# Attention and mixture of experts in one kernel: where the next head pair's q, k and v are moved, split and loaded

## The chip, the cores and the metric

The kernel runs on one core of a Trainium2 chip. The metric is the device time of one execution in microseconds (us), less is better. TensorE is PE in the profile, with its weight loads apart as PEld; VectorE is DVE, ScalarE is ACT, GpSimd is POOL, and SyncE is SP, whose queue (SPq) issues nearly all the DMAs.

## The reference

Attention over 2 batches of 8 heads, with 1152 keys of 64 values; queries are first averaged in twos, to 576 per head. Its output, as 1152 rows of 512, goes through 4 experts that are weighted with given probabilities.

```python
def _attn_ref(q, k, v):
    q_pool = q.reshape(B, H, S // 2, 2, D).mean(axis=3)
    scores = scale * np.matmul(q_pool, k.transpose(0, 1, 3, 2))
    attn = np.exp(scores - np.max(scores, axis=-1, keepdims=True))
    attn = attn / (np.sum(attn, axis=-1, keepdims=True) + 1e-09)
    return np.matmul(attn, v)
...
    p = domain_probs / (domain_probs.sum(-1, keepdims=True) + 1e-09)
    for e in range(E):
        h = np.maximum(x @ w1[e], 0.0)
        out += p[:, e:e + 1] * (h @ w2[e])
```

All is float32. Products that need more than one pass of TensorE take their operands as a rounded part (hi) and the rest (lo), each a tile of its own.

## The kernel before

**Pairs and periods.** Attention goes through 8 pairs of heads, n = 0 to 7. A pair has 9 tiles of 128 queries, and the program's main loop has one period for each, i = 0 to 8 (g = 9n + i counts them through). A period transposes one tile of exponentials (`T_chunk`, PE writes `pt`, DVE and ACT copy it to `aT`), does a part of the product with v (`PV_part`, PE writes `po`), and computes the scores of a tile that is three ahead (`scores`, PE writes `spt`; two ahead in pair 0), whose maximum DVE takes at once (L356) and whose exponentials ACT makes (L362). So the first scores of pair n+1 are computed in period 6 of pair n. Tile 8 holds the last 64 queries of both heads, and its scores are 9 matmuls of 384 columns (L327); the others' are L345 from pair 1 on, and read both halves of the partitions at once.

**Preparing a pair.** While pair n runs, pair n+1 is made ready, and pair n+2 is loaded:

- `load_q`, `load_kv` load q, k and v from HBM (SPq L169, L173).
- `add_q` adds neighbouring queries on POOL, `join_k` copies k to where it is transposed from (POOL L263).
- `prep_q` transposes q and the last eighth of k (PE writes `pq`), ACT copies them to `raw`, and POOL splits them into hi and lo (`pool_split`, L209 and L210): first the four full tiles, to a staging tile `stq`, then `split_q2m`, q's last tile, in four operations of 64 x 64, then k's. `move_q` takes each half of `stq` to the partitions where the scores read it, with two DMAs (SPq L282).
- `prep_k` does the same for k in two parts, `c` = 1 and 2 (PE writes `pk`); `stack_k` copies each to the other half of the partitions, two DMAs for each part (SPq L274, `kk<-kk`).

In pairs 1 and later `prep_k` stands in periods 1 and 3, `prep_q` in period 8 (for n+2); in pair 0 they stand in periods 3 to 5.

**x.** In periods 3 and 8 a product with v is complete. `finish` scales it on DVE (L428, tile `xr`) and splits the result on POOL for the experts (`xa` or `xb`), which read it after all pairs.

**Order.** All engines run their instructions in the order in which the program writes them, and so does the SP queue, where each wait holds up what stands behind it. In `S_rows` one matmul of a tile must be finished before another starts, and this is passed on by an empty instruction on SP (`relay`, L349) in every full tile from g = 13.

Of the kernel before, what the change touches and what calls it, by code (L numbers as in the profile page):

```python
# [8 lines left out]
F32 = mybir.dt.float32  # L9
F32R = mybir.dt.float32r  # L10
AF = mybir.ActivationFunctionType
ALU = mybir.AluOpType
# [5 lines left out]
def attention_moe_kernel(ctx, tc, q, k, v, probs, w1, w2, out):  # L18
    nc = tc.nc
    B, H, S, D = q.shape  # L20
    NT, DM = out.shape
    E, _, FF = w1.shape
    P = 128
    HALF = 64
# [40 lines left out]
    def xop(op, z, kt):  # L65
        if op in ("A11", "A12"):
            return xa[:, int(op == "A12"), z, kt, :]
        j = XI[op]
        if kt == 0:
            return xb[:, j, z, :]  # L70
        if j < 4 or z == 0:
            return q2all[:, (2 * j + z) * HT:(2 * j + z + 1) * HT]
        return kk[0][:, 3584:3584 + HT]
# [69 lines left out]
    with ExitStack() as actx:  # L143
# [12 lines left out]
        pr = ap.tile([P, 2 * 9, E], F32, name="pr")  # L156
        prs = ap.tile([P, 2 * 9], F32, name="prs")

        for t in q2m:
            nc.gpsimd.memset(t[:HALF, :, HALF:].bitcast(F32), 0.0)  # L160
            nc.gpsimd.memset(t[HALF:, :, :HALF].bitcast(F32), 0.0)

        pairs = [(b, hp) for b in range(B) for hp in range(NPAIR)]
        NP = len(pairs)
# [18 lines left out]
        def add_q(eng):  # L183
            eng.tensor_tensor(
                qsum[:, :8].rearrange("p (j y) d -> p y j d", y=2),
                qn[:, :8, 0, :].rearrange("p (y j) d -> p y j d", y=2),
                qn[:, :8, 1, :].rearrange("p (y j) d -> p y j d", y=2), ALU.add)
            eng.tensor_tensor(
                qsum[:, 8:], qn[:, 8:, 0, :].to_broadcast([P, 2, D]), qn[:, 8:, 1, :].to_broadcast([P, 2, D]), ALU.add)

        TCH = [(0, 5), (5, 9)]
        ROWS = [slice(0, HALF), slice(HALF, P)]
# [15 lines left out]
        def pool_split(hi, lo, src):  # L208
            nc.gpsimd.tensor_scalar(hi, src, 1.0, 1.0, ALU.mult, ALU.mult)  # L209
            nc.gpsimd.tensor_tensor(lo, src, hi.bitcast(F32), ALU.subtract)  # L210
# [11 lines left out]
        def prep_q0():  # L222
            pt = transposes_q0(range(4, 9))
            src = raw[:, :10 * HALF].rearrange("p (a k x) -> p a k x", a=2, x=HALF)
            nc.vector.tensor_copy(src, pt)
            pool_split(*parts_q0(1), src[:, :, :4])
            split_q2m(0, src)

        def split_q2m(n, src):
            for a, r in enumerate(ROWS):  # L230
                pool_split(q2m[n % 2][r, 0, r], q2m[n % 2][r, 1, r], src[r, a, 4])

        def half_of(h, z):
            return z if h else 1 - z
# [49 lines left out]
        def prep_q(n):  # L284
            pt = half_transposes("pq", [qsum[:, 2 * j:2 * j + 2].rearrange("p t d -> p (t d)") for j in range(5)] + [kc[0]])
            src = raw[:, :6 * P].rearrange("p (a k x) -> p a k x", a=2, x=HALF)
            nc.scalar.activation(src, pt, AF.Copy)
            pool_split(stq[:, 0], stq[:, 1], src[:, :, :4])
            if n == 1:
                for y in range(2):  # L290
                    move_q(n, y)
            split_q2m(n, src)
            ab = kab[n % 2]
            pool_split(halves(ab[:, 0], 8, 9)[:, :, 0], halves(ab[:, 1], 8, 9)[:, :, 0], src[:, :, 5])

# [126 lines left out]
        def finish(n, grp, po):  # L422
            b, hp = pairs[n]
            w, kt = GW[grp], hp % 2
            c = slice(256 * grp, 256 * grp + w)
            c1 = slice(HT + 256 * grp, HT + 256 * grp + w)
            x = xr[:, hp, c1 if b else c]
            nc.vector.tensor_tensor(x, po[:, :w], rb[grp], ALU.mult)  # L428
            if b == 0:
                op = "A12" if hp > 1 else "A11"  # L430
                pool_split(xop(op, 0, kt)[:, c], xop(op, 1, kt)[:, c], x)
                return
            a11, a12, a21 = xr[:, kt, c], xr[:, kt + 2, c], xr[:, kt, c1]
            if hp < 2:
                nc.gpsimd.tensor_tensor(a11, a11, x, ALU.subtract)
                if hp == 0:
                    split_x("S3", 0, c, a11, nc.gpsimd)
                return
            eng = nc.vector if hp == 3 else nc.gpsimd
            eng.tensor_tensor(a11, x, a11, ALU.subtract)  # L440
            todo = [("S2", a11), ("S1", a21), ("A22", x), ("S4", a12)]
            if eng is nc.gpsimd:
                eng.tensor_tensor(a21, a21, x, ALU.add)
                eng.tensor_tensor(a12, a12, a11, ALU.subtract)
                for op, src in todo:
                    split_x(op, kt, c, src, eng)
                return
            hi, lo = split_parts(todo[0], kt, c)
            hi()
            eng.tensor_tensor(a21, a21, x, ALU.add)  # L450
            eng.tensor_tensor(a12, a12, a11, ALU.subtract)
            rest = [split_parts(t, kt, c) for t in todo[1:]]
            late.append([lo] + [r[1] for r in rest])
            late.append([r[0] for r in rest])
            if grp == 0:
                for fn in late.pop() + late.pop():
                    fn()
# [5 lines left out]
                    lambda: nc.vector.tensor_tensor(lo, src, hi.bitcast(F32), ALU.subtract))  # L463

        late = []

        def scores(g):
            if g < NTL:
# [43 lines left out]
                 4: (0, 0, 0, 2), 5: (0, 0, 2, 4), 6: (0, 0, 4, 6), 7: (0, 0, 6, 8), 8: (0, 0, 8, 9)}  # L512
        SPREAD = {7: (0, 0), 2: (-1, 1)}
        PREP = {1: [(prep_k, 1)], 3: [(prep_k, 2)]}
        PREP0 = {3: [(prep_q,)], 4: [(prep_k, 1)], 5: [(prep_k, 2)]}

        def pv_part(g):
            n, i = divmod(g, 9)
# [18 lines left out]
        for g in range(NTL):  # L537
            n, i = divmod(g, 9)
            if i == 6 and n + 2 < NP:
                add_q(nc.gpsimd)  # L540
                join_k(0)
            if i == 7 and n + 2 < NP:
                join_k(1)
            if g == 2:
                load_q(2)
            if g == NTL - 1:
                nc.scalar.activation(UT["m1"], chx[:, :2, :CW], AF.Copy)
            for c in range(2):
                T_chunk(g, c)
            if g <= NQT:  # L550
                exps(g + 1)
            if i == 0 and n:
                inv_sums(n - 1, 1)
            if i == 4:
                inv_sums(n, 0)
            if g == NTL - 1:
                inv_sums(n, 1)
            if NQT < g < NTL - 2 and i not in (3, 8):
                exps(g + 2)
            if g == NQT:  # L560
                PV_part(0, 1, 0, 1)
                scores(g + 2)
                exps(g + 2)
                PV_part(0, 1, 1, 3)
            else:
                pv_part(g)
            if i in SPREAD and n + SPREAD[i][0] >= 0:
                spread_sums(n + SPREAD[i][0], SPREAD[i][1])
            if g == 0:
                prep_q0()  # L570
            if n + 1 < NP:
                for fn, *args in (PREP if n else PREP0).get(i, []):
                    fn(n + 1, *args)
                if i == 8 and n + 2 < NP:
                    prep_q(n + 2)
                if g == 5:
                    load_kv(kn, k, 2)
            elif i == 7:
                chx = ps_s.tile([P, 3, 512], F32, tag="s", name="chx")
                for kt in range(2):  # L580
                    product(0, 0, kt, chx, True)
            elif i == 8:
                for kt in range(2):
                    product(0, 2, kt, chx, False)
            if NQT <= g < NTL - 2 and i in (3, 8):
                exps(g + 2)
            scores(g + 2 if g < NQT else g + 3)
            if n and n + 1 < NP:
                if i == 0 and n + 2 < NP:
                    load_q(n + 2)  # L590
                if i in (1, 3):
                    move_q(n + 1, i // 2)
                if i in (2, 4):
                    stack_k(n + 1, *KST[i // 2 - 1])
                if i == 2 and n + 2 < NP:
                    load_kv(kn, k, n + 2)
                if i == 5:
                    load_kv(vn[(n + 1) % 2], v, n + 1)
            if g == 0:
                stack_k0()  # L600
                add_q(nc.gpsimd)
                join_k(0)
                join_k(1)
            if (n, i) == (1, 4):
                gate_weights()
            if (n, i) == (NP - 2, 4):
                load_w1(0)
            if (n, i) == (NP - 2, 7):
                w1_sums(0)
            if n == NP - 1:  # L610
                if i == 0:
                    split_x("S3", 1, slice(0, HT), xr[:, 1, :HT], nc.gpsimd)
                    load_w2(0)
                if i < 4:
                    w1_hi(0, WCH[i:i + 1])
                    w1_lo(0, WCH[i:i + 1])
                if i == 3:
                    load_w1(1)
                if i == 5:
                    w1_sums(1)  # L620
# [156 lines left out]
```

## Time and profile before

| | |
|---|---|
| Time, median of 3 runs | 632.39 us (630.92 to 633.32) |
| The profiled execution | 632.08 us, of which the span from first to last instruction is 629.9 us |
| PE busy | 608.2 us (97% of the span) |
| POOL busy | 346.9 us (55%) |
| DVE, ACT busy | 370.2 us, 292.9 us |
| DMAs on the SP queue | 48.94 MB |

Attention takes about the first 259 us of the span, the experts the rest. Times of rows are counted from the first instruction. The profiled execution is one, and its time lies 0.31 us under the median.

### The profile page before, as it was taken

What the parts mean: (1) busy time and instruction counts of PE and PEld (TensorE: products, weight loads), DVE (VectorE), ACT (ScalarE), POOL (GpSimd) and SP (SyncE); (2) the same over time, 40 slices, a digit from 0 to 9 for tenths busy, and PEclk for the clock granted to TensorE, in tenths of its full rate; (3) what the DMA queues carried; (4) which work ended last, traced back from release to release, by engine and by line L of the source; (5) the groups of instructions that cost most, each with busy time, mean ns of one, the idle gap of its engine ahead of it and who ended that gap; (6) DMA issues with size and microseconds to landing.
All of it is one profiled execution on the core that took longest, in us unless ns stands there. A gap on an engine that the chain in (4) does not pass through costs nothing.

```text
span 629.9 us, 12429 instructions
## 1 busy us (share of the span) xinstructions
PE 608.2 (97%) x5036; PEld 512.0 (81%) x5036; DVE 370.2 (59%) x571; ACT 292.9 (47%) x467; POOL 346.9 (55%) x415
## 2 busy tenths in 40 slices
PE   7889999999999999999999999999999999999997
PEld 6667677676777776889989989989989989989975
DVE  6657787786868777554454454454454454454444
ACT  5656667666667773635235235235225235224120
POOL 2655364543546498686476476476467467467040
PEclk8999999999999999999999999999999999999999
DMA  6574574928363521121121121121111111110105
GB/s 225 133 202 114 107 185 111 208 75 192 92 167 87 129 69 35 33 68 35 34 67 34 36 66 33 41 62 33 47 56 35 50 51 34 50 51 2 34 0 151
DMA packets 41337, 50.91 MB, mean 81 GB/s; under 512 B 3264, under 2 KB 27072, under 8 KB 41280
## 3 DMA queue, kind: packets, MB, share of 16 engines
q1 hardware_dynamic: 40480, 48.94, 29.9%
q10 hardware_dynamic: 800, 1.18, 0.5%
q8 instruction: 40, 0.66, 0.5%
q14 instruction: 17, 0.14, 0.1%
HBM read 30.97 MB, written 2.36 MB: 53 GB/s over the span
## 4 chain that ended last, share of the span: by engine, by line
PE 80%; DVE 6%; DMA 5%; POOL 3%; issue 2%; ACT 2%; SPq 0%; DVEq 0%; ACTq 0%
PE p L733 31%; PE chy L135 11%; PE chx L135 8%; PE chz L135 8%; PE po L391 7%; PE spt L345 7%; PE pt L202 4%; DMA kk<-kk 4%; DVE sx L356 3%; PE spt L327 2%; DMA kq<-in_k_dram 1%; POOL kk L210 1%; PE pq L202 1%; PE pr L202 1%; POOL kk L209 1%
## 5 line engine op out<-in xcount | busy, mean ns | idle before, releaser
L733 PE MATMUL p<-w2s,hb 128*128 128x512 f32 (+1 forms) x870 | 199.2, 388 | 1.1 <-DVE acc L737 0.9
L733 PEld LDWEIGHTS p<-w2s,hb 128*128 128x128 f32 x870 | 161.7, 188 | 34.3 <-issue 1.3
L737 DVE SCALAR_TENSOR_TENSOR acc<-p,pw,acc 128x512 f32<-128x512 f32 (+1 forms) x136 | 101.5, 747 | 82.7 <-PE p L733 82.7
L116 POOL TENSOR_TENSOR kk<-kq,kk 128x512 fp32r<-128x512 f32 x64 | 72.4, 1160 | 117.8 <-ACT kk L108 117.8
L356 DVE TENSOR_SCALAR_CACHE_REDUCE sx<-spt 128x1152 f32<-128x1152 f32 x72 | 97.7, 1357 | 53.6 <-PE spt L345 25.2
L362 ACT ACTIVATE sx<-sx,mn 128x1152 f32<-128x1152 f32 x72 | 90.5, 1257 | 22.5 <-DVE sx L356 22.4
L391 PE MATMUL po<-aT,vn 128*64 128x320 f32 (+1 forms) x576 | 85.5, 418 | 0.0
L664 POOL TENSOR_TENSOR hb<-xr,hb 128x576 fp32r<-128x576 f32 x48 | 68.7, 1433 | 21.9 <-ACT hb L663 21.9
L701 ACT ACTIVATE xr<-chx 128x576 f32<-128x576 f32 x15 | 9.8, 651 | 147.5 <-PE chx L135 147.5
L345 PE MATMUL spt<-kk,q2all 64*128 64x512 f32 (+1 forms) x504 | 65.1, 366 | 5.7 <-DMA kk<-kk 4.8
L345 PEld LDWEIGHTS spt<-kk,q2all 64*128 64x128 f32 x504 | 54.5, 186 | 18.5 <-DVE sx L356 6.4
L378 ACT ACTIVATE aT<-pt 128x640 f32<-128x640 f32 x72 | 50.5, 701 | 39.1 <-PE pt L202 39.0
L202 PEld LDWEIGHTS pt<-ident,sx 64*128 64x128 f32 x1296 | 55.5, 141 | 5.7 <-issue 3.5
L202 PE MATMUL pt<-ident,sx 64*128 64x64 f32 x1296 | 59.1, 227 | 0.5 <-ACT xr L304 0.4
L135 PE MATMUL chx<-xa,kk 128*128 128x288 f32 x384 | 56.5, 296 | 0.8 <-ACT xr L701 0.5
L135 PEld LDWEIGHTS chx<-xa,kk 128*128 128x128 f32 x384 | 53.4, 188 | 2.8 <-issue 0.9
L391 PEld LDWEIGHTS po<-aT,vn 128*64 128x64 f32 x576 | 35.0, 136 | 19.8 <-issue 0.2
L376 DVE COPY aT<-pt 128x512 f32<-128x512 f32 x72 | 49.3, 685 | 2.6 <-PE pt L202 2.6
L95 POOL TENSOR_TENSOR kq<-kq 128x256 f32<-128x256 f32 x64 | 45.8, 736 | 7.8 <-DMA kq<-in_moe_w_dram 6.7
L662 ACT ACTIVATE xr<-xr 128x576 f32<-128x576 f32 x48 | 32.9, 685 | 34.1 <-DVE xr L660 34.0
L135 PE MATMUL chy<-xb,kk 128*128 128x288 f32 x288 | 46.6, 297 | 0.5 <-ACT xr L670 0.3
L135 PE MATMUL chy<-q2all,kk 128*128 128x288 f32 x256 | 44.1, 294 | 0.0
(105 smaller groups left out, 726.9 us busy)
## 6 DMA issues: line engine op xcount, KB each, us to landing
kq<-in_moe_w_dram SPq DMA_DIRECT2D x64, 128.0 KB, 2.4
qsf<-in_moe_w_dram SPq DMA_DIRECT2D x16, 512.0 KB, 3.7
q2all<-q2all SPq DMA_DIRECT2D x28, 256.0 KB, 4.1
vn<-in_v_dram SPq DMA_DIRECT2D x8, 576.0 KB, 6.6
kk<-kk SPq DMA_DIRECT2D x14, 320.0 KB, 6.0
kq<-in_q_dram SPq DMA_DIRECT2D x7, 576.0 KB, 3.7
kq<-in_k_dram SPq DMA_DIRECT2D x7, 576.0 KB, 6.9
kk<-kk SPq DMA_DIRECT2D x14, 256.0 KB, 3.8
```

The lines of the kernel that those rows point to most:

```text
L116: nc.gpsimd.tensor_tensor(flat(w1s[u % 2][:, 1, a:b]), flat(wf[:, a:b]), flat(w1s[u % 2][:, 0, a:b].bitcast(F32)), ALU.subtract)
L135: nc.tensor.matmul(chain[:, c, :CW], w1s[u % 2][:, a, WI[wo], kt, :], xop(xo, z, kt)[:, c * CW:(c + 1) * CW], start=(first and kt == 0 and ...
L202: nc.tensor.transpose(pt[:, a, j, :], src[r], ident[r, r])
L345: mm = nc.tensor.matmul(sp[:, cs[c]], q2[n % 2][r, zq, h, ts_], src[n % 2][r, zk, cs[c]], start=(zq + zk == 0), stop=(zq == 1), skip_group ...
L356: nc.vector.tensor_scalar(sx[g % 3].rearrange("p (c x) -> p c x", c=3), spt.pop(g), -INV, None, ALU.mult, ALU.min, accum_out=mn[g % 3])
L362: nc.scalar.activation(sx[g % 3], sx[g % 3], AF.Exp, bias=mn[g % 3], scale=-1.0, accum_out=sums[n % 2][:, i:i + 1])
L376: nc.vector.tensor_copy(dst, pt)
L378: nc.scalar.activation(dst, pt, AF.Copy)
L391: nc.tensor.matmul(po[h * HALF:(h + 1) * HALF, :w], vn[n % 2][:, h, kt, :], aT[grp][:, h, kt, :], start=(kt == 0), stop=(kt == KT - 1))
L664: nc.gpsimd.tensor_tensor(lo, c, hi.bitcast(F32), ALU.subtract)
L733: nc.tensor.matmul(pc, h[:, a, sl, ts_], w[:, b, sl, c0:c1], start=(m == 0), stop=(m == len(ops) - 1))
L737: nc.vector.scalar_tensor_tensor(ac, pc, pw[:, tt, e:e + 1], ac, ALU.mult, ALU.add)
```

## The change

Four things are written in another order, and one is computed otherwise.

1. Where the result is split for the experts on POOL, `finish` puts it into a list, `behind`, that the main loop empties after the period's `prep_q` or `prep_k`. The last two heads' own path, on DVE, stays where it was.
2. `move_q` stands in periods 0 and 1 (before: 1 and 3), the first ahead of `load_q`; k of pair n+2 is loaded in period 4, behind the second `stack_k` (before: period 2, behind the first). `join_k(0)` is written in period 7.
3. `split_q2m` is gone: `add_q` writes the last tile's sums only into the half where they belong, the other half is set to zero once in `prep_q0`, and one split of 128 x 128 writes q's last tile with its zeros. Two of the four memsets at the start go.
4. In pair 0, `prep_q` and both `prep_k` stand in periods 2, 3 and 4.

```diff
-            eng.tensor_tensor(
-                qsum[:, 8:], qn[:, 8:, 0, :].to_broadcast([P, 2, D]), qn[:, 8:, 1, :].to_broadcast([P, 2, D]), ALU.add)
+            for a, r in enumerate(ROWS):
+                eng.tensor_tensor(qsum[r, 8 + a], qn[r, 8, 0, :], qn[r, 8, 1, :], ALU.add)
...
-            split_q2m(0, src)
-
-        def split_q2m(n, src):
             for a, r in enumerate(ROWS):
-                pool_split(q2m[n % 2][r, 0, r], q2m[n % 2][r, 1, r], src[r, a, 4])
+                pool_split(q2m[0][r, 0, r], q2m[0][r, 1, r], src[r, a, 4])
+                nc.gpsimd.memset(qsum[r, 9 - a], 0.0)
...
-            split_q2m(n, src)
+            pool_split(*(q2m[n % 2][:, z].rearrange("p (a x) -> p a x", a=2) for z in range(2)), src[:, :, 4])
...
-                pool_split(xop(op, 0, kt)[:, c], xop(op, 1, kt)[:, c], x)
+                behind.append(lambda: pool_split(xop(op, 0, kt)[:, c], xop(op, 1, kt)[:, c], x))
...
-                nc.gpsimd.tensor_tensor(a11, a11, x, ALU.subtract)
+                behind.append(lambda: nc.gpsimd.tensor_tensor(a11, a11, x, ALU.subtract))
...
-        PREP0 = {3: [(prep_q,)], 4: [(prep_k, 1)], 5: [(prep_k, 2)]}
+        PREP0 = {2: [(prep_q,)], 3: [(prep_k, 1)], 4: [(prep_k, 2)]}
...
             if i == 6 and n + 2 < NP:
                 add_q(nc.gpsimd)
+            if i == 7 and n + 2 < NP:
                 join_k(0)
-            if i == 7 and n + 2 < NP:
                 join_k(1)
...
+            while behind:
+                behind.pop(0)()
             if NQT <= g < NTL - 2 and i in (3, 8):
                 exps(g + 2)
             scores(g + 2 if g < NQT else g + 3)
             if n and n + 1 < NP:
+                if i < 2:
+                    move_q(n + 1, i)
                 if i == 0 and n + 2 < NP:
                     load_q(n + 2)
-                if i in (1, 3):
-                    move_q(n + 1, i // 2)
                 if i in (2, 4):
                     stack_k(n + 1, *KST[i // 2 - 1])
-                if i == 2 and n + 2 < NP:
+                if i == 4 and n + 2 < NP:
                     load_kv(kn, k, n + 2)
                 if i == 5:
                     load_kv(vn[(n + 1) % 2], v, n + 1)
```

The SP queue through one pair (n = 2) before: q's load, the first half of q's move, the first part of k's, k's load, q's second half, k's second part, v's load.

```order
L169 DMA kq<-in_q_dram 128x1152
L282 DMA q2all<-q2all 64x4x256 x2
L274 DMA kk_74<-kk_74 64x2x512 x2
L173 DMA kq<-in_k_dram 128x2x576
L282 DMA q2all<-q2all 64x4x256 x2
L274 DMA kk_74<-kk_74 64x2x640 x2
L173 DMA vn_89<-in_v_dram 128x2x576
```

The same stretch after (the changed file's lines are a few lower):

```order
L279 DMA q2all<-q2all 64x4x256 x2
L168 DMA kq<-in_q_dram 128x1152
L279 DMA q2all<-q2all 64x4x256 x2
L271 DMA kk_74<-kk_74 64x2x512 x2
L271 DMA kk_74<-kk_74 64x2x640 x2
L172 DMA kq<-in_k_dram 128x2x576
L172 DMA vn_89<-in_v_dram 128x2x576
```

All eight moves now stand ahead of the loads of k and v.

POOL in periods 1 to 4 of the same pair before: k's first part is joined and split (`kk`, hi and lo), then the result of the pair before for the experts (`xa`), then k's second part, and `spread`, which serves the sums of the exponentials.

```order
L263 COPY qsf<-kq 128x512
L209 TENSOR_SCALAR kk_74<-raw 128x512
L210 TENSOR_TENSOR kk_74<-raw,kk_74 128x512
L209 TENSOR_SCALAR xa<-xr 128x320
L210 TENSOR_TENSOR xa<-xr,xa 128x320
L209 TENSOR_SCALAR kk_74<-raw 128x512
L210 TENSOR_TENSOR kk_74<-raw,kk_74 128x512
L402 COPY spread<-rs_104 128x256
```

And after:

```order
L260 COPY qsf<-kq 128x512
L208 TENSOR_SCALAR kk_74<-raw 128x512
L209 TENSOR_TENSOR kk_74<-raw,kk_74 128x512
L208 TENSOR_SCALAR kk_74<-raw 128x512
L209 TENSOR_TENSOR kk_74<-raw,kk_74 128x512
L208 TENSOR_SCALAR xa<-xr 128x320
L209 TENSOR_TENSOR xa<-xr,xa 128x320
L399 COPY spread<-rs_104 128x256
```

The two operations on `xa` moved from ahead of k's second split to behind it.

PE in pair 0 before, from the transposes (`pt`) of period 2 on: q's preparation (`pq`) in period 3, k's first part (`pk`) in period 4, its second further on.

```order
L202 MATMUL pt<-ident,sx_92 128x64 x18
L327 MATMUL spt<-kk_73,q2all 128x384 x6
L202 MATMUL pt<-ident,sx_90 128x64 x18
L202 MATMUL pq<-ident,qsf 128x64 x10
L202 MATMUL pq<-ident,raw 128x64 x2
L327 MATMUL spt<-kk_73,q2all 128x384 x6
L202 MATMUL pt<-ident,sx_91 128x64 x18
L391 MATMUL po<-aT_93,vn_88 64x256 x4
L202 MATMUL pk<-ident,qsf 128x64 x8
L327 MATMUL spt<-kk_73,q2all 128x384 x6
```

And after, from the same transposes on:

```order
L201 MATMUL pt<-ident,sx_92 128x64 x18
L201 MATMUL pq<-ident,qsf 128x64 x10
L201 MATMUL pq<-ident,raw 128x64 x2
L324 MATMUL spt<-kk_73,q2all 128x384 x6
L201 MATMUL pt<-ident,sx_90 128x64 x18
L201 MATMUL pk<-ident,qsf 128x64 x8
L324 MATMUL spt<-kk_73,q2all 128x384 x6
L201 MATMUL pt<-ident,sx_91 128x64 x18
L388 MATMUL po<-aT_93,vn_88 64x256 x4
L201 MATMUL pk<-ident,qsf 128x64 x8
```

Each of the three preparations moved up by one period; the number of PE's instructions is the same.

## Rows read from the trace of the kernel before

**Rows 1.** Windows: length, busy us of five engines, clock, DMA share, GB/s.
```profile
12.60:45.22 32.62, 27.90 (x314) 21.27 (x315) 20.30 (x33) 20.19 (x30) 16.73 (x29) 0.91 0.74 191
62.87:91.63 28.76, 27.40 (x358) 20.36 (x355) 22.77 (x42) 19.24 (x30) 14.51 (x27) 1.00 0.60 139
91.63:118.82 27.19, 26.97 (x358) 20.24 (x355) 22.25 (x39) 19.22 (x30) 13.74 (x24) 1.00 0.62 149
118.82:147.32 28.50, 27.37 (x358) 20.36 (x355) 22.27 (x39) 19.25 (x30) 13.82 (x24) 1.00 0.60 145
147.32:176.42 29.10, 27.59 (x357) 20.44 (x354) 21.54 (x39) 19.21 (x30) 14.38 (x25) 1.00 0.59 138
176.42:204.87 28.45, 27.37 (x358) 20.37 (x355) 21.37 (x39) 19.25 (x30) 14.10 (x22) 1.00 0.48 110
```

**Rows 2.** Waits of PE: for whom, us in total, times, longest.
```profile
PE spt L345 <- DMA kk<-kk: 4.8, 5, 1.3
...
PE pq L202 <- POOL raw L263: 1.1, 1, 1.1
```

**Rows 3.** Timeline of pair 4, periods 3 to 8.
```profile
144.03 0.60 ACT L304 ACTIVATE raw<-pk 128x512 f32<-128x512 f32 x1 [1.22 <-PE pk L202]
144.31 0.46 POOL L209 TENSOR_SCALAR xa<-xr 128x320 fp32r<-128x320 f32 x1 [3.63 <-DVE xr L428]
144.85 0.87 POOL L210 TENSOR_TENSOR xa<-xr,xa 128x320 fp32r<-128x320 f32 x1
145.69 0.63 POOL L209 TENSOR_SCALAR kk<-raw 128x512 fp32r<-128x512 f32 x1
146.39 1.13 PE L345 MATMUL spt<-kk,q2all 64*128 64x512 f32 x9
146.40 1.29 POOL L210 TENSOR_TENSOR kk<-raw,kk 128x512 fp32r<-128x512 f32 x1
146.85 0.86 DVE L400 TENSOR_SCALAR rs<-sums 128x4 f32<-128x4 f32 x1
147.71 1.24 SPq L274 DMA_DIRECT2D kk<-kk  x2
149.27 1.51 PE L327 MATMUL spt<-kk,q2all 128*128 128x384 f32 x7 [0.16 <-DVE sx L356]
...
154.56 1.06 PE L345 MATMUL spt<-kk,q2all 64*128 64x128 f32 x8 [1.29 <-DMA kk<-kk]
159.94 0.25 PE L202 MATMUL pq<-ident,raw 64*128 64x64 f32 x2
```

**Rows 4.** DMAs from 141 us to 149.5 us, pair 4.
```profile
DMA packets 1323, 1.88 MB, mean 221 GB/s; under 512 B 97, under 2 KB 798, under 8 KB 1322
...
kk<-kk SPq DMA_DIRECT2D x2, 320.0 KB, 7.1
kq<-in_k_dram SPq DMA_DIRECT2D x1, 576.0 KB, 7.6
...
kk<-kk SPq DMA_DIRECT2D x2, 256.0 KB, 3.6
```

**Rows 5.** Timeline of pair 5: the same DVE operation, and POOL's beside it.
```profile
175.77 0.62 POOL L209 TENSOR_SCALAR kk<-raw 128x512 fp32r<-128x512 f32 x1
175.99 0.42 DVE L400 TENSOR_SCALAR rs<-sums 128x4 f32<-128x4 f32 x1
```

**Rows 6.** Timeline of pair 0.
```profile
21.04 0.29 POOL L263 COPY raw<-kq 128x128 f32<-128x128 f32 x1
21.72 1.31 PE L327 MATMUL spt<-kk,q2all 128*128 128x384 f32 x6 [0.80 <-DVE sx L356]
...
37.76 1.00 SPq L173 DMA_DIRECT2D kq<-in_k_dram  x1
43.97 0.29 POOL L263 COPY raw<-kq 128x128 f32<-128x128 f32 x1 [5.86 <-DMA kq<-in_k_dram]
44.31 0.28 PE L202 MATMUL pq<-ident,raw 64*128 64x64 f32 x2 [1.11 <-POOL raw L263]
```

More of the change, by code (lines that the diff above doesn't have):

```diff
@@ L157, in attention_moe_kernel @@
         prs = ap.tile([P, 2 * 9], F32, name="prs")
-        for t in q2m:
-            nc.gpsimd.memset(t[:HALF, :, HALF:].bitcast(F32), 0.0)
-            nc.gpsimd.memset(t[HALF:, :, :HALF].bitcast(F32), 0.0)
+        nc.gpsimd.memset(q2m[0][:HALF, :, HALF:].bitcast(F32), 0.0)
+        nc.gpsimd.memset(q2m[0][HALF:, :, :HALF].bitcast(F32), 0.0)
         pairs = [(b, hp) for b in range(B) for hp in range(NPAIR)]
@@ L434, in finish, with sums, all_split @@
             if hp < 2:
-                nc.gpsimd.tensor_tensor(a11, a11, x, ALU.subtract)
+                behind.append(lambda: nc.gpsimd.tensor_tensor(a11, a11, x, ALU.subtract))
                 if hp == 0:
-                    split_x("S3", 0, c, a11, nc.gpsimd)
+                    behind.append(lambda: split_x("S3", 0, c, a11, nc.gpsimd))
                 return
-            eng = nc.vector if hp == 3 else nc.gpsimd
-            eng.tensor_tensor(a11, x, a11, ALU.subtract)
             todo = [("S2", a11), ("S1", a21), ("A22", x), ("S4", a12)]
-            if eng is nc.gpsimd:
+            def sums(eng):
                 eng.tensor_tensor(a21, a21, x, ALU.add)
                 eng.tensor_tensor(a12, a12, a11, ALU.subtract)
+            def all_split(eng):
+                eng.tensor_tensor(a11, x, a11, ALU.subtract)
+                sums(eng)
                 for op, src in todo:
                     split_x(op, kt, c, src, eng)
+            if hp == 2:
+                behind.append(lambda: all_split(nc.gpsimd))
                 return
+            nc.vector.tensor_tensor(a11, x, a11, ALU.subtract)
             hi, lo = split_parts(todo[0], kt, c)
             hi()
-            eng.tensor_tensor(a21, a21, x, ALU.add)
-            eng.tensor_tensor(a12, a12, a11, ALU.subtract)
+            sums(nc.vector)
             rest = [split_parts(t, kt, c) for t in todo[1:]]
@@ L465, in attention_moe_kernel @@
         late = []
+        behind = []
         def scores(g):
```

## The prediction

> **What bounds the kernel now.** I read the windows first. Cut from period 5 of one pair to period 5 of the next, the five stretches do the same work, and PE is busy for 27.0 us to 27.6 us in each. But only one lasts as little as 27.19 us; the others last 28.76, 28.50, 29.10 and 28.45 us, all at full clock [rows 1]. So PE bounds attention, and four pairs hold 1.3 us to 1.9 us more than PE's work. The waits of PE say what that is: five waits for `kk<-kk`, the second part of k's move to the other half of the partitions, and one for POOL's copy L263 in front of q's preparation [rows 2]. The experts behind are 370 us of nearly unbroken matmuls that none of the edits touches: what attention saves should come off the end.
>
> Pair 4 shows how the wait arises [rows 3]. ACT delivers k's transposed second part at 144.63 (144.03 + 0.60). POOL is then busy with `xa`, which nobody needs before the experts, and takes k up at 145.69; its lo part ends at 147.69, and the SP queue issues the move at 147.71. PE, in period 6, starts the next pair's first tile and finds the move missing from 153.27 to 154.56. The move is not only issued late, it is slow: the two DMAs of k's second part took 7.1 us, while the two of its first part, 256 KB instead of 320 KB, took 3.6 us [rows 4]. What differs is what was issued ahead of them: k's load of 576 KB and q's second half.
>
> **The change part by part.**
>
> *Split and loads behind k's move.* With `xa` behind it, k's split can begin at 144.63, 1.06 us sooner, and ends at 146.63. The issue gains less: SP first has to pass on a matmul of the tile that starts at 146.39 and ends at 147.52 [rows 3]; I take 147.0. Ahead of this move there is now only k's first part, two periods older. Its transfer is bounded below by the 3.6 us of the smaller moves and above by 7.1 us; I take 4.5 us, which is 3.6 x 320 / 256, since nothing else is in flight ahead of it. It lands at 151.5, 1.8 us before PE asks, and the wait goes whole. What comes next in that place is known from the one stretch without it: 27.19 us [rows 1]. The gain is the excess over that stretch: 1.57 + 1.31 + 1.91 + 1.26 = 6.05 us. Bounds: 0 and 6.05.
>
> [...]
>
> *q moved in periods 0 and 1, q loaded behind its first half.* The same number of DMAs, each of which now waits at SP only for a split that POOL has finished about then; behind it in the queue stand empty instructions that PE waits for. Two DMAs take SP 1.24 us to issue, in a period of some 3 us (27.19 / 9) [rows 1, 3]. I cost it at nothing; if POOL were late by a microsecond PE would lose what exceeds the rest of the period, so 0 to +1 us over the kernel.
>
> *q's last tile in two operations instead of four, two additions instead of one.* All on POOL, which is busy for 14 us of 27 us in a pair [rows 1], and away from the path once `xa` is behind. Nothing.
>
> *A small DVE operation.* `rs` (L400), four columns wide, took 0.86 us in pair 4, from 146.85 to 147.71, beside POOL's lo operation that ended at 147.69; in pair 5, beside a shorter POOL operation, it took 0.42 us and ended as that one did [rows 3, 5]. Behind it PE waits 0.16 us for DVE [rows 3]. Pairs 1 to 4 have this pattern. With k's lo finished at 146.63, `rs` meets `xa`'s first operation (0.46 us) and should take about 0.42 us. That frees 0.16 us of PE four times: 0.64 us. Bounds: 0, and 0.44 x 4 = 1.8 us.
>
> *Pair 0.* Preparing a period earlier ends two waits: the pair's wait for `kk<-kk`, one of five that make 4.8 us, so about 1.0 us, and the wait of 1.11 us for POOL's copy, which waited 5.86 us for k's load [rows 2, 6]. That load was issued at 37.76 behind the moves; with them a period (3 us) sooner it lands before the copy is asked for. There is a price: in period 2 q's transposes now stand ahead of the scores that started at 21.72, and POOL's copy that they need ended at 21.33 (21.04 + 0.29) [rows 6]. Two memsets and a second addition come ahead of that copy. From POOL's other small operations I take 0.8 us, so the transposes (0.28 us) end near 22.4 and the scores start 0.7 us late; some of it comes back in period 5, which loses a preparation. I take 0.5 us. Sum for pair 0: 1.0 + 1.1 - 0.5 = 1.6 us gained; bounds 0 and 2.6.
>
> *The sum.* 6.05 + 0.64 + 1.6 = 8.3 us. Against the profiled execution's 632.08 us that is 623.8 us; the median of the runs is 0.31 us above that execution, so I say **624.0 us**.
>
> **The rivals.**
>
> *The moves stay half as slow.* If transfers share the engines whatever their order, k's load (1.3 us behind) and v's take a part from the moves. The 640 KB of the moves would have 1.3 us alone at 221 GB/s (0.29 MB), and the other 0.37 MB at half to a third of the rate, 3.3 us to 5.0 us; with the 1.2 us that 3.6 us holds beyond 512 KB at that rate, that is 5.8 us to 7.5 us, a landing at 152.8 to 154.5, and up to 1.2 us of the wait stays in four pairs. [...] Time: 625 to 628.8, in the middle 627.
>
> *DVE caught behind `xa`.* [...] If `rs` gets its turn only after both `xa` operations, 146.63 + 0.46 + 0.87 = 147.96, it ends 0.3 us later than before instead of 0.4 us sooner [rows 3]; with the 0.16 us not gained, four pairs lose 1.8 us: 625.8. Against it: in pair 5 it got in directly behind one operation, with another waiting [rows 5].
>
> *k comes too late: slower.* k's load is now issued about 148.3 in pair 4. PE transposes the copy from it at 159.94, or about 158.2 without the wait, so it must land by 157.7, 9.4 us after its issue. Before it took 7.6 us; moves, k and v together, 1.84 MB at 221 GB/s, take 8.3 us from 147.0, plus 1.2 us: 156.5 even if k lands last [rows 3, 4]. If it took 12 us, PE would wait 2.6 us in each of five pairs: 632.1 - 8.3 + 13 = 637. It makes the kernel slower than before from 1.7 us a pair, a transfer of 11.1 us.
>
> [...]
>
> *The wait only changes its name*, another engine being as late in period 6: 630 to 632. The 27.19 us speak against it.
>
> **How the numbers follow.** Forecast 0.66 (622 to 625.7 with its own bounds), moves half as slow 0.14, DVE behind `xa` 0.08, k too late 0.05, clock 0.03, wait renamed 0.04. The range from 622.0 to 629.0 leaves out the two that end above it and a part of the forecast's lower end. A measurement of this kernel can tell about 0.5% (3.2 us) from no change: faster 0.87, same 0.08, slower 0.05.
>
> **What would show it.** PE's waits for `kk<-kk` gone in pairs 1 to 5, with all five stretches at 27.0 us to 27.3 us; k's second move landing in about 4.5 us, and issued at the end of POOL's lo operation or with the tile in flight; `rs` near 0.4 us; no wait for POOL's L263 in pair 0, and some 0.7 us more in its period 2. I am wrong if PE waits for POOL's L263 in period 8, which would be k's load, or if the moves still take 6 us.

## The result, and the profile after

The changed kernel takes 620.78 us (median of 6 runs, 619.88 to 621.99), the one before, run beside it, 630.29 us (6 runs, 627.36 to 633.32): a ratio of 0.9851 [0.9817, 0.9885]. The direction and the places were as forecast. The time is 1.2 us below the stated range, which began at 622.0.

The profiled execution took 621.87 us with a span of 619.8 us, against 632.08 and 629.9 us before: 10.1 us less. Windows of the changed kernel, as in [rows 1]: pair 0, then from period 5 of one pair to period 5 of the next (length, busy us of PE, PEld, DVE, ACT, POOL, clock, DMA share, GB/s):

```profile
12.24:42.72 30.48, 27.23 (x317) 20.83 (x317) 20.10 (x33) 19.84 (x30) 16.63 (x30) 0.94 0.79 187
60.18:87.20 27.02, 26.96 (x357) 20.28 (x354) 21.46 (x42) 19.26 (x30) 14.33 (x26) 1.00 0.61 150
87.20:114.21 27.01, 26.95 (x357) 20.27 (x354) 20.90 (x39) 19.24 (x30) 13.54 (x23) 1.00 0.60 150
114.21:141.23 27.02, 26.96 (x357) 20.28 (x354) 20.91 (x39) 19.25 (x30) 13.54 (x23) 1.00 0.59 150
141.23:168.24 27.01, 26.95 (x357) 20.28 (x354) 20.93 (x38) 19.24 (x30) 14.25 (x23) 1.00 0.60 150
168.24:195.30 27.06, 27.00 (x357) 20.28 (x354) 21.25 (x39) 19.25 (x30) 14.01 (x23) 1.00 0.50 128
```

All five stretches now last as long as PE works in them, to 0.06 us. Together they take 135.12 us, where those of [rows 1] add up to 142.00: 6.88 us. Pair 0 gives 2.14 us (32.62 less 30.48). The other 1.1 us lies where nothing was forecast: 0.36 us ahead of pair 0 (12.60 less 12.24), 0.19 us between pair 0 and the first stretch, 0.5 us behind the last.

The waits of PE, the four longest groups of twelve, none of which is for `kk<-kk` (for whom, us in total, times, longest):

```profile
PE warm L488 <- POOL ident masks.py:199: 1.4, 1, 1.4
PE pq L201 <- POOL qsf L183: 1.0, 1, 1.0
PE p L739 <- DVE acc L743: 0.9, 1, 0.9
PE spt L324 <- DVE sx L353: 0.8, 1, 0.8
```

The 4.8 us of [rows 2] are gone, and so is the wait for POOL's copy of k. New is the second line: in pair 0's period 2, q's transposes now wait for POOL's additions (`qsf`, L183). The timeline of pair 4, to be laid beside [rows 3] (start, duration, engine, line, operation, idle before it and for whom):

```profile
137.95 0.60 ACT L301 ACTIVATE raw<-pk 128x512 f32<-128x512 f32 x1 [1.23 <-PE pk L201]
138.63 0.62 POOL L208 TENSOR_SCALAR kk<-raw 128x512 fp32r<-128x512 f32 x1 [4.05 <-ACT raw L301]
139.34 1.28 POOL L209 TENSOR_TENSOR kk<-raw,kk 128x512 fp32r<-128x512 f32 x1
140.32 1.14 PE L342 MATMUL spt<-kk,q2all 64*128 64x512 f32 x9
140.58 0.47 POOL L208 TENSOR_SCALAR xa<-xr 128x320 fp32r<-128x320 f32 x1
140.78 0.29 DVE L397 TENSOR_SCALAR rs<-sums 128x4 f32<-128x4 f32 x1
140.99 1.24 SPq L271 DMA_DIRECT2D kk<-kk  x2
...
142.28 0.99 SPq L172 DMA_DIRECT2D kq<-in_k_dram  x1
143.39 1.31 SPq L172 DMA_DIRECT2D vn<-in_v_dram  x1
146.49 1.13 PE L342 MATMUL spt<-kk,q2all 64*128 64x512 f32 x9
148.73 0.29 POOL L260 COPY raw<-kq 128x128 f32<-128x128 f32 x1 [4.47 <-DMA kq<-in_k_dram]
151.95 0.26 PE L201 MATMUL pq<-ident,raw 64*128 64x64 f32 x2
```

POOL takes up k's transposed part 0.08 us after ACT has written it (138.55), and the `xa` operations stand behind. The move is issued at 140.99 with PE's scores of 146.49 still 5.5 us away. Its length is in the view of the DMAs of the same pair, from 135.43 us to 144.77 us (KB each, median us from issue to landing); the rows beside it are in [rows 4]:

```profile
kk<-kk SPq DMA_DIRECT2D x2, 320.0 KB, 4.1
kq<-in_k_dram SPq DMA_DIRECT2D x1, 576.0 KB, 6.3
...
kk<-kk SPq DMA_DIRECT2D x2, 256.0 KB, 5.2
```

The move took 4.1 us instead of 7.1 us. The smaller one, which now has q's load and q's second half close ahead of it, rose from 3.6 to 5.2 us, and nobody waits for it.

### The profile page after: what moved, and what is told of

It is laid out like the page before. It is cut to its first block, busy times and chain, and to the rows that moved or that the text cites. A ratio compares the mean times of both kernels' runs of the same rounds, so it can differ in the third digit from the quotient of the medians.

```text
span 619.8 us, 12418 instructions
## 1 busy us (share of the span) xinstructions
PE 607.1 (98%) x5036; PEld 512.5 (83%) x5036; DVE 365.8 (59%) x571; ACT 293.1 (47%) x467; POOL 345.4 (56%) x408
## 3 DMA queue, kind: packets, MB, share of 16 engines
HBM read 30.97 MB, written 2.36 MB: 54 GB/s over the span
## 4 chain that ended last, share of the span: by engine, by line
PE 91%; DVE 3%; ACT 2%; issue 1%; POOL 1%; DMA 0%; SPq 0%; DVEq 0%; POOLq 0%; ACTq 0%
PE p L739 32%; PE chy L135 12%; PE po L388 11%; PE spt L342 8%; PE chx L135 8%; PE chz L135 8%; PE pt L201 6%; PE spt L324 4%; DVE sx L353 1%; PE pk L201 1%; PE pr L201 1%; ACT sx L359 1%; PE pq L201 1%; DMA kq<-in_k_dram 0%; DVE q2all L466 0%
## 5 line engine op out<-in xcount | busy, mean ns | idle before, releaser
L342 PE MATMUL spt<-kk,q2all 64*128 64x512 f32 (+1 forms) x504 | 63.2, 365 | 0.6 <-DVE sx L353 0.6
L201 PE MATMUL pt<-ident,sx 64*128 64x64 f32 x1296 | 57.6, 226 | 0.3 <-ACT raw L284 0.2
```

The lines of the kernel that those rows point to most:

```text
L201: nc.tensor.transpose(pt[:, a, j, :], src[r], ident[r, r])
L342: mm = nc.tensor.matmul(sp[:, cs[c]], q2[n % 2][r, zq, h, ts_], src[n % 2][r, zk, cs[c]], start=(zq + zk == 0), stop=(zq == 1), skip_group ...
```

## The experiments

**Each part of the change by itself.** Four kernels, each the one before with one part. First the SP order alone, with `join_k(0)` in period 7, as in the changed kernel:

```diff
                 add_q(nc.gpsimd)
-                join_k(0)
             if i == 7 and n + 2 < NP:
+                join_k(0)
                 join_k(1)
...
+                if i < 2:
+                    move_q(n + 1, i)
                 if i == 0 and n + 2 < NP:
                     load_q(n + 2)
-                if i in (1, 3):
-                    move_q(n + 1, i // 2)
-                if i == 2 and n + 2 < NP:
+                if i == 4 and n + 2 < NP:
                     load_kv(kn, k, n + 2)
```

> The kernel before with only the SP queue in the new order (q moved in periods 0 and 1, k loaded behind the second part of k's move, join_k(0) written in period 7). Theory (the transfer is slow because loads stand ahead of it in the queue): the move is issued as late as before, behind xa and k's split, but takes 3.6 to 4.5 us instead of 5.4 to 6.8, lands before PE asks, and all four waits of pairs 1 and 3 to 5 go: 6.0 us less, 0.9905. The operation rs stays at 0.86 us in pairs 1 to 4, and PE still waits 0.16 us behind it. Rival (the issue is too late, whatever stands ahead; loads behind share the engines): the move still takes 5.5 us or more, and 0.5 us or more of each wait stays: 2 to 4 us less, 0.994 to 0.997.

Measured: 623.38 us, ratio 0.9875 [0.9843, 0.9907]. Timeline, DMAs (136.73 to 146.24 us) and the windows of the same pair, period 5 and period 6:

```profile
142.05 0.86 DVE L400 TENSOR_SCALAR rs<-sums 128x4 f32<-128x4 f32 x1
142.91 1.24 SPq L274 DMA_DIRECT2D kk<-kk  x2
```

```profile
kk<-kk SPq DMA_DIRECT2D x2, 320.0 KB, 4.1
```

```profile
142.49:146.24 3.75, 3.59 (x40) 2.67 (x37) 2.50 (x5) 2.48 (x5) 2.44 (x4) 1.00 0.52 116
146.24:148.91 2.67, 2.67 (x36) 2.07 (x37) 1.97 (x3) 1.78 (x2) 0.00 (x0) 1.00 0.99 280
```

The move is issued as late as before, 3.08 us after period 4's start (142.91 less 139.83; before 147.71 less 144.63), and yet takes 4.1 us, and period 6 has no wait. So the order of the SP queue took the wait away by itself; which part of that order did it is tried further down. `rs` still takes 0.86 us.

The second, `xa`'s splits behind k's and nothing else:

```diff
-                pool_split(xop(op, 0, kt)[:, c], xop(op, 1, kt)[:, c], x)
+                behind.append(lambda: pool_split(xop(op, 0, kt)[:, c], xop(op, 1, kt)[:, c], x))
...
+            while behind:
+                behind.pop(0)()
             if NQT <= g < NTL - 2 and i in (3, 8):
```

> The kernel before with only the splits of x behind those of k and q on POOL. Theory: the move is issued 0.7 us to 1.0 us sooner but still takes 6 us to 7 us behind k's load and q's second half, so each of the four waits loses only that 0.7 us to 1.0 us and 0.2 us to 0.6 us of PE's wait stays: 3 to 4 us less; rs falls to some 0.3 to 0.4 us in pairs 1 to 4 and 0.2 us of each period 5 goes: 0.8 us less; together 4 to 5 us, 0.992 to 0.994. Rival (the issue time is all that counts): all waits gone, 7 us less, 0.989.

Measured: 631.17 us, ratio 1.0007 [0.9974, 1.0041], so no part of the gain that I had expected of it. Pair 4, first the timeline, then PE's waits in the whole kernel, then its DMAs from 139.51 to 148.83 us:

```profile
143.40 1.28 POOL L210 TENSOR_TENSOR kk<-raw,kk 128x512 fp32r<-128x512 f32 x1
144.64 0.46 POOL L209 TENSOR_SCALAR xa<-xr 128x320 fp32r<-128x320 f32 x1
144.84 0.29 DVE L400 TENSOR_SCALAR rs<-sums 128x4 f32<-128x4 f32 x1
145.03 1.24 SPq L274 DMA_DIRECT2D kk<-kk  x2
...
151.91 1.07 PE L345 MATMUL spt<-kk,q2all 64*128 64x128 f32 x8 [0.87 <-DMA kk<-kk]
```

```profile
PE spt L345 <- DMA kk<-kk: 4.6, 5, 1.5
```

```profile
kk<-kk SPq DMA_DIRECT2D x2, 320.0 KB, 7.3
```

The move is issued 2.41 us after period 4's start (142.62) instead of 3.08, 0.67 us sooner, and takes 0.2 us longer; this pair's wait shrank from 1.29 to 0.87 us, pair 3's grew from 0.90 to 1.49 us, and over the pairs the waits still add up to 4.6 us. In pairs 1 to 5 the first DMA of the move was issued 0.67 us sooner (1.6 us in pair 5) and landed, counted from period 4's start, 0.2 us sooner on average (9.1 us instead of 9.3), from 0.65 us sooner in pair 4 to 0.4 us later in pair 3. Behind the load most of an earlier issue was lost. What did change is `rs`: it took 0.29 us instead of 0.86 us, and period 5 went from about 3.75 to about 3.55 us in pairs 1 to 4. The 0.8 us which that makes are too few to show in the times.

The third and fourth are pair 0's preparation a period earlier, and q's last tile in two operations (the split is shown; its sums and memsets are as in the changed kernel):

```diff
-        PREP0 = {3: [(prep_q,)], 4: [(prep_k, 1)], 5: [(prep_k, 2)]}
+        PREP0 = {2: [(prep_q,)], 3: [(prep_k, 1)], 4: [(prep_k, 2)]}
```

> The kernel before with only pair 0's preparation in periods 2 to 4. Theory: pair 0 loses its two waits (k's move, POOL's copy in front of q's transposes) and pays about half a microsecond in period 2: 1.6 to 2.2 us less, 0.9965 to 0.9975; the waits of pairs 1 to 5 stay. Rival (TensorE's clock falls in the idle time that period 2 then has, and takes the gain back): within 1 us of before, with a stretch at half clock after period 2.

```diff
-            split_q2m(n, src)
+            pool_split(*(q2m[n % 2][:, z].rearrange("p (a x) -> p a x", a=2) for z in range(2)), src[:, :, 4])
```

> The kernel before with only q's last tile zeroed by its sums and split in two operations. Theory: POOL is off the path there, so within 0.5 us of before, 1.000. Rival (POOL's time in period 8 and 0 counts): 0.6 us of POOL in each of six pairs comes off, up to 3.6 us, 0.994.

Measured: 630.10 us, 0.9978 [0.9952, 1.0005], and 630.11 us, 0.9988 [0.9959, 1.0016]. In the timing neither can be told from nothing. The first one's trace shows pair 0 at 30.74 us where it was 32.62, with a granted clock of 0.50 in period 0 of both (4.63 us long); the second's shows PE's waits for `kk<-kk` as before, 5.9 us. Pair 0 of the first:

```profile
12.59:43.33 30.74, 27.80 (x316) 21.48 (x315) 20.17 (x33) 19.65 (x30) 16.79 (x29) 0.91 0.78 203
```

**The order undone piece by piece.** In the changed kernel, `xa` back ahead of k's split (the list emptied before the period's preparations):

> The changed kernel with x's splits back ahead of those of k and q on POOL. Theory (after the run with the new SP order alone): the move is issued about 1 us later but still lands before PE asks, so no wait for it; only rs takes 0.86 us again in pairs 1 to 4, 0.2 us a pair, so 0.8 us more than the changed kernel, 0.986. Rival (both halves of the edit are needed): waits of 0.5 us or more come back, 0.990 or above.

Measured: 621.40 us, ratio 0.9836 [0.9787, 0.9885]: not to be told from the changed kernel. There is no wait for the move, which takes 4.0 to 4.3 us; what it loses is 0.18 us in a pair:

```profile
139.87 0.85 DVE L397 TENSOR_SCALAR rs<-sums 128x4 f32<-128x4 f32 x1
```

```profile
113.11:140.31 27.20, 26.99 (x358) 20.27 (x355) 22.24 (x39) 19.25 (x30) 13.62 (x23) 1.00 0.58 149
```

Then the loads: v's load alone in period 3, ahead of the second part of k's move; k's load directly ahead of it; and k's and v's both.

```diff
+                if i == 3:
+                    load_kv(vn[(n + 1) % 2], v, n + 1)
                 if i in (2, 4):
                     stack_k(n + 1, *KST[i // 2 - 1])
...
-                if i == 5:
-                    load_kv(vn[(n + 1) % 2], v, n + 1)
```

> The changed kernel with one difference: v's load (576 KB) stands in period 3, ahead of the second part of k's move, instead of behind it. The move is issued when it was, and POOL's order is the changed one. Theory (what counts is the load that stands ahead in the queue): the move takes 6 us to 7 us instead of 3.7 us, and PE waits for it 0.3 us to 1.2 us in each of pairs 1 to 5 again: 0.990 to 0.993 of the kernel before. Rival (k's load as such, or POOL's order, made the wait): no wait, 0.985 as the changed kernel.

```diff
-                if i in (2, 4):
-                    stack_k(n + 1, *KST[i // 2 - 1])
                 if i == 4 and n + 2 < NP:
                     load_kv(kn, k, n + 2)
+                if i in (2, 4):
+                    stack_k(n + 1, *KST[i // 2 - 1])
```

> The changed kernel with two statements of period 4 exchanged: k's load (576 KB) is issued directly ahead of the second part of k's move instead of directly behind it; all else as changed. Theory (transfers are served in the order of the queue, so what stands ahead is paid): the move is issued 0.7 us later and takes 6 us to 7 us instead of 3.7 us, and PE waits for it 0.7 us to 1.8 us in each of pairs 1 to 5, those with a load of k: 4 to 9 us more than the changed kernel, 0.991 to 0.999. Rival (transfers share the engines whatever their order; the load 0.65 us ahead or behind is the same): the move takes at most 1 us longer, no wait of over 0.3 us, 0.985 to 0.987.

> The same with v's load also ahead of the move: 1152 KB ahead instead of 576 KB. Theory: as k_first with another 2.5 us to 3 us for the second load, so waits of 3 us to 5 us in pairs 1 to 5 (and some 2 us in pair 6, which loads v alone); long waits may bring TensorE's clock down behind them, as in pairs 3 and 4 of the second profile of the kernel before. Time 640 to 655 us. Rival (shared): no more than k_first.

Measured: v ahead 622.13 us (4 runs), 0.9870 [0.9813, 0.9928]. Its profile is that of its fastest run (620.60 us) and has no wait, against the theory; the slowest took 626.57 us at a mean clock of 0.988, and whether PE waited there isn't known. v's load was issued 2.7 us ahead of the move, which took 4.2 to 5.6 us. I take it that too little of the load was left by then; no run shows how much, so this kernel doesn't decide between theory and rival.

k directly ahead: 629.25 us (11 runs), 0.9964 [0.9935, 0.9992]. That is about three quarters of the gain lost by exchanging two neighbours in the queue, with the same bytes: in pair 4 the move was issued 0.4 us later in its period than in the changed kernel, and k's load 0.5 us ahead of it instead of 1.3 us behind. Its profile is that of its fastest run (624.31 us), and even there PE waits 1.34 us in pair 1 and about 0.5 us in pairs 2, 3 and 5; what a run of 629 us looks like is not on record. PE's waits, and the DMAs in pair 4 from 136.52 to 145.83 us:

```profile
PE spt L342 <- DMA kk<-kk: 2.9, 4, 1.3
```

```profile
kk<-kk SPq DMA_DIRECT2D x2, 320.0 KB, 5.9
kq<-in_k_dram SPq DMA_DIRECT2D x1, 576.0 KB, 4.4
```

k's load fell from 6.3 to 4.4 us and the move rose from 4.1 to 5.9 us (7.2 us in pair 1): of the two, the one issued first gained and the other lost. With both ahead, one run took 651.02 us, PE's waits, and then pair 4's periods 6 and 7:

```profile
PE spt L342 <- DMA kk<-kk: 15.6, 6, 2.8
```

```profile
159.09:164.63 5.54, 3.08 (x37) 2.17 (x37) 1.97 (x3) 2.05 (x3) 0.85 (x2) 0.98 0.76 181
164.63:168.93 4.30, 4.30 (x43) 3.09 (x42) 2.39 (x4) 2.05 (x3) 0.00 (x0) 0.63 0.02 4
```

The bytes ahead doubled, and the loss against the changed kernel went from 8.5 us (medians) to 30.2 us (one run). A second price came with it: behind a wait of 2.46 us the granted clock was 0.63 (0.98 in the period with the wait), and the period behind took 4.30 us instead of 2.75. In pair 3, behind a wait of 2.82 us, it was 0.50 from 131 to 135 us.

**The same price in the kernel before.** A second profile of it:

> The kernel before, unchanged, for a second profile. Its runs lie between 627.4 us and 633.3 us, wider than the changed kernel's 619.9 us to 622.0 us. Theory (the waits for the move and the place at which the clock falls in pair 0 vary between executions): the waits of single pairs differ from those of the first profile by up to 1 us, the fall at 11 us to 18 us may be missing (1.5 us to 2 us less in pair 0), and the stretches without a wait are again 27.2 us. Rival (the engines' work itself varies): these stretches differ too.

It took 635.12 us. Pair 4's periods 6 and 7, and then the two stretches with the longest waits, to be laid beside the fourth and fifth line of [rows 1]:

```profile
153.38:158.46 5.08, 3.03 (x37) 2.12 (x37) 1.97 (x3) 2.05 (x3) 0.84 (x2) 0.98 0.80 185
158.46:162.77 4.31, 4.31 (x42) 3.05 (x41) 2.39 (x4) 2.05 (x3) 0.00 (x0) 0.62 0.02 8
```

```profile
118.95:149.62 30.67, 28.91 (x358) 21.23 (x355) 22.35 (x39) 19.24 (x30) 13.79 (x24) 0.94 0.55 132
149.62:181.04 31.42, 29.15 (x357) 21.34 (x354) 21.65 (x39) 19.23 (x30) 14.39 (x25) 0.95 0.54 130
```

The wait here was 2.05 us, where [rows 3] had 1.29, and behind it the granted clock was 0.62. In pair 3 it fell behind 1.54 us (0.94 in that stretch; the profile puts that wait down to v's load; the move's first DMA landed at 126.32, and PE went on at 126.46). In pair 1 it did not behind 1.16 us (1.00 in that stretch), and in pairs 2 and 5 PE hardly waited. The move took 7.0 to 7.5 us in pairs 1, 3 and 4 and 4.5 us in pair 5. So the wait differs from run to run, and the longer ones are paid twice: the five stretches take 145.43 us here, where those of [rows 1] took 142.00. Pair 0's period 0 was slow again (4.63 us, granted clock 0.50). The times of the kernel before vary accordingly: the 10 runs beside this experiment go from 629.98 to 637.15 us, and the slowest has the lowest mean clock (0.985). The seven of the changed kernel lie within 2.7 us.

**Pair 0.** Three runs for the new wait in period 2: a second profile of the changed kernel; three transposes, whose result is not used, added in each of periods 0 to 2, against the fall of the clock there (0.50 from 21 to 24.3 us in the changed kernel's first profile, behind a wait of 1.0 us); and POOL's additions for pair 1 and its first copy of k written ahead of pair 0's own splits, against the wait.

> The changed kernel again, for a second profile. Theory (the fall of the clock in its pair 0 comes in some executions only): no fall, period 2 4.2 us instead of 5.26 us and period 3 3.07 us instead of 3.33 us, pair 0 29.2 us instead of 30.5 us; pairs 2 to 6 at 27.0 us as in its first profile, no wait for k's move. Rival (the fall belongs to the changed kernel): pair 0 30.5 us again.

> The changed kernel with three transposes of the identity more in each of periods 0, 1 and 2 of pair 0, in time in which PE waited; their result is not used. [...] Theory (the fall follows PE's idle time in these periods): no fall, period 2 takes 3.3 us to 3.8 us, pair 0 28.5 us to 29.3 us instead of 30.47 us, 1.2 us to 2 us less than the changed kernel: 0.982 to 0.983. Rival (the fall comes by chance in any execution, or the transposes cost what they save): as the changed kernel, 0.985.

```diff
+            for a, r in enumerate(ROWS):
+                nc.gpsimd.memset(qsum[r, 9 - a], 0.0)
+            add_q(nc.gpsimd)
+            join_k(0)
             pool_split(*parts_q0(1), src[:, :, :4])
...
-                nc.gpsimd.memset(qsum[r, 9 - a], 0.0)
...
                 stack_k0()
-                add_q(nc.gpsimd)
-                join_k(0)
                 join_k(1)
```

> The changed kernel with POOL's additions for pair 1 and the first copy of its k moved ahead of the splits of pair 0's second half of q. In the changed kernel's period 2 PE waits about 1 us for POOL's additions in front of q's transposes, and 0.4 us more between them. Theory (POOL stood idle until 15.1 us, and the splits that now come later are asked for only at about 19 us): this wait goes, period 2 takes 3.1 us to 3.4 us instead of 4.2 us, 0.8 us to 1.1 us less than the changed kernel, 0.983 to 0.984. Rival (the scores of period 2 then wait for the split as long as q's transposes did for the additions): as the changed kernel, 0.985.

Measured: 619.35 us (one run, profiled), 621.06 us, 0.9830 [0.9795, 0.9864], and 620.92 us, 0.9823 [0.9787, 0.9858]. None of the kernels differs measurably from the changed one. Period 2 in the changed kernel's first and second profile:

```profile
18.28:23.54 5.26, 4.10 (x36) 3.14 (x36) 1.97 (x3) 2.87 (x4) 4.08 (x9) 0.76 0.94 199
```

```profile
17.00:21.23 4.23, 3.04 (x36) 2.31 (x36) 1.97 (x3) 2.86 (x4) 3.23 (x8) 1.00 1.01 205
```

In the first profile the granted clock was 0.50 from 21 us on, behind the wait of 1.0 us; in the second it stayed at 1.00, behind the same wait, and pair 0 took 29.17 us instead of 30.48. With the added transposes it stayed at 1.00 too, but period 2 took 4.21 us, where I had expected 3.3 to 3.8, and pair 0 29.16 us: just what the second profile has without them, so nothing shows that they did it. Early additions take period 2 to 3.19 us, and yet pair 0 is only some 0.2 us shorter (28.93 us), because periods 5, 7 and 8 grow in turn.

## Why the prediction was right in mechanism and wrong in size

**The wait of four pairs** (6.05 us, and 0.64 us for `rs`, 6.69 us together): between the two profiled executions the five stretches lost 6.88 us. Most of the difference is in the last stretch, which I had compared with 27.19 us, although it has no slow `rs` and takes 27.06 us without a wait. The transfer was put at 4.5 us and took 4.1 to 4.8 us. It was to land 1.8 us before PE asks; the first of its two DMAs, which is the one that this tile reads, landed at 144.59 us (140.99 + 3.61), 1.9 us before the tile starts at 146.49. That what is issued behind a move takes little from it was my estimate; the runs show 4.1 us in pair 4 with k's load directly behind, and 5.9 us there (6.4 to 7.2 us in the other pairs) with it directly ahead.

**What did the work.** I had put the split behind and the loads behind into one term. The runs part them: the SP order alone gives 0.9875, the split alone 1.0007. That k's split starts 1 us sooner, and that the move is issued 0.6 to 0.7 us sooner, was worth next to nothing in either order: ahead of the loads the move has 1.9 us to spare, and with the loads ahead of it the move landed 0.2 us sooner on average. The split's own worth is `rs`: 0.2 us in each of four pairs, 0.8 us where I said 0.64. `rs` took 0.29 us; the rival that had it caught behind both `xa` operations is refuted, as it ended at 141.07, between the first of them (to 141.05) and the second (from 141.13).

**Pair 0 was mis-sized, and near by luck.** I said 1.6 us (1.0 + 1.1 - 0.5); the profiles measured 2.14 us, each with a fall of the clock, in period 0 before and in period 2 after. Like with like it is 1.9 us with period 0 slow in both (32.62, and 30.74 for pair 0's change alone), and 1.8 us with no fall in either (30.97 for the SP order alone, 29.17 for the second profile of after). But the parts were wrong. The 1.0 us for the pair's wait was the mean of five; pair 0's own was 0.50 us in the trace that I read:

```profile
40.45 1.01 PE L345 MATMUL spt<-kk,q2all 64*128 64x512 f32 x8 [0.50 <-DMA kk<-kk]
```

The price in period 2 was 1.36 us (4.23 us against 2.87 in the SP order alone) where I took 0.7 us of delay, and the profile that I read hid it. In that profile period 0 of pair 0 had a granted clock of 0.50 and lasted 4.63 us; at 1.00 it took 3.11 us in the changed kernel's first profile and 3.13 us in the SP order alone. So PE came to period 2 at 20.14 us, and POOL's copy, at 21.04 [rows 6], was 0.9 us away. With PE in time the copy is 1.85 us away in the SP order alone (period 2 from 18.33 us) and 2.43 us in the second profile of after (from 17.00 us), 0.58 us more, for the memsets and the second addition:

```profile
20.18 0.28 POOL L263 COPY raw<-kq 128x128 f32<-128x128 f32 x1
```

```profile
19.43 0.29 POOL L260 COPY raw<-kq 128x128 f32<-128x128 f32 x1
```

In the kernel with pair 0's change alone, whose period 0 was slow again, period 2 grew by only 0.32 us, to 3.19. What made up for both errors is that k's two preparations fitted into periods 3 and 4 without making them longer (3.06 and 3.36 us in the second profile of after, 3.19 and 3.48 in the SP order alone), while periods 5 to 8 gave back more than the two waits: 12.48 us against 15.39.

**The step that failed is the sum's first term, taken from one execution.** The price of the wait was read from a single profile, 6.05 us (6.69 with `rs`), and 6.05 was also set as the most that it could be. Four profiles are of kernels with the old SP order and `xa` ahead: the first and second of the kernel before, pair 0's change alone, and q's last tile alone. Their five stretches take 6.9, 10.3, 8.0 and 7.4 us more than the changed kernel's 135.12 us, 8.15 us on average, and the profile that I read is the lowest of the four. (Four are few, and the average is rough.) What was left out is that the wait varies, and that behind the longer ones the clock falls (0.62 behind 2.05 us). The times say the same. The median that I started from, 632.39 us, was of three runs; with three more it is 630.29 us, later series of the same kernel gave 631.10 (29 runs), 631.45 (10) and 631.95 us (16), and all 61 together 631.67 us. From there to 620.78 is 10.9 us, and my sum was 8.3.

Two smaller steps failed with it. What I put at nothing, the time outside the five stretches and pair 0, gave 1.1 us in the two profiles: 0.36 us at the start, which moves by more than that between two profiles of the changed kernel (12.24 and 10.98 us), 0.19 us ahead of the first stretch, and 0.5 us behind attention, where the time from the last scores to the end goes from 394.0 to 394.8 us over all fourteen profiles; what sets it stays open. And the range was cut at 622.0, although its own upper bounds, 6.05 + 1.8 + 2.6, reached 621.6 from the execution's time; nothing in it stood for the spread between executions.

**The rivals.** Moves half as slow for shared engines: refuted, 4.1 to 4.8 us with 1152 KB issued behind. k too late: refuted, it landed at 148.6 (142.28 + 6.33), POOL copied it at 148.73, and PE needed it at 151.95; I had left 1.2 us, it was some 3 us. Wait renamed: refuted by the waits of PE. The clock (0.03), another fall of it in pair 0's period 2: it came in one of the changed kernel's two profiles, 0.50 from 21 to 24.3 us, and pair 0 was 1.3 us longer there.

## What to carry to other kernels

Where a short on-chip move and long loads share a queue, issue the move first and the loads behind it, whenever the loads have slack: here exchanging two neighbours of one queue was worth 7 to 8.5 us of 630 (ratios of 0.9964 and 0.9851, medians of 629.25 and 620.78 us). Ask of a late transfer first what is queued ahead of it, then when it is issued; here an earlier issue behind the load gained next to nothing. And when a wait that varies is to be removed, take its price from several executions, with what comes behind it.

## What the runs showed of the hardware

Two things I had not expected. Behind a load of 576 KB most of what a move gained by an earlier issue was lost again, 0.7 of 0.9 us on average over five pairs: with `xa`'s splits behind and nothing else changed, it was issued 0.67 us sooner and took 0.1 to 0.2 us longer in pairs 1, 2 and 4 and 1.1 us longer in pair 3 (7.8 us where it was 6.7); in pair 5 it was issued 1.6 us sooner and took 1.6 us longer. PE's waits still came to 4.6 us.

And TensorE's granted clock was lower behind the longer waits for this move. The second profile of the kernel before has two, of 1.54 and 2.05 us, and that of k and v ahead has six, 15.6 us together, the longest 2.8 us. The periods behind those of 2.05 and 2.46 us took 4.31 and 4.30 us instead of 2.75, at 0.62 and 0.63 (the rows above); the stretches of pairs 3 and 4 in the one profile had 0.94 and 0.95, those of pairs 1 to 5 in the other 0.90 to 0.95. Stretches with shorter waits had 1.00, also that with the wait of 1.49 us in the kernel with `xa`'s splits behind. In the first profile of the kernel before the periods behind waits of 0.90 to 1.29 us took 2.83 to 2.87 us. In pair 0 these runs show no such order. Six profiles have the same wait of 1.0 us in period 2; the clock fell behind it in two (0.50 from 21 to 24.3 us in the changed kernel's first, and from 22 to 24 us with k and v ahead) and was 1.00 in four. Period 0 had 0.50 and 4.63 us in three profiles of fourteen, both of the kernel before and that of pair 0's change alone. What decided it stays open.
